# Three causal selects per head group, unscaled values and a newly searched instruction order in a gated attention and FFT kernel

## Chip, cores and metric

The kernel runs on one core of a Trainium2 chip. The metric is the device time of one execution, in microseconds (us), as the median of several runs. Three runs of the kernel before took 241.19, 241.27 and 241.69 us, a median of 241.27 us.

## The reference

The output is a mix of two branches over the same input rows (2048 tokens of 640 values). Branch A is attention in four segments of 512 tokens with 32 heads of 20 values; each segment attends causally to itself and reads a memory that the earlier segments have written. Branch B multiplies a two-dimensional FFT of the rows by weights. Cut to what matters:

```python
g = _sigmoid(beta).reshape(1, H, 1, 1)          # one gate per head
for s in range(N):                              # 4 segments of L = 512
    logits = einsum('bhqd,bhkd->bhqk', qs, ks) * Dh ** -0.5 + mask
    a_dot = einsum('bhqk,bhkd->bhqd', softmax(logits), vs)
    num = einsum('bhld,bhde->bhle', phi(qs), M)
    den = einsum('bhld,bhd->bhl', phi(qs), z)[..., None] + 1e-06
    o = g * (num / den) + (1.0 - g) * a_dot     # phi(t) = t + 1 if t > 0 else exp(t)
    M = M + einsum('bhld,bhle->bhde', phi(ks), vs)
    z = z + einsum('bhld->bhd', phi(ks))
a = concat(o) @ wo
b = irfft2(rfft2(x) * (w_r + 1j * w_i))
t = _sigmoid((x * gate_w).sum(-1))              # one gate per token
return t * a + (1 - t) * b
```

## The kernel before

**How the program is made.** `Kern.record()` writes down every operation with what it reads and writes; nothing is sent to an engine yet. `Sched.schedule` then goes through a long table of numbers, ORDER, which holds each engine's queue (so the order on TensorE, VectorE, ScalarE, GpSimd and SyncE is written by hand, or rather by a search), and gives the PSUM banks out while it walks along. Where an operation may run on two engines (`copy_alts`: ScalarE or VectorE, `either` and `small`: VectorE or GpSimd), the table also chooses the engine. A second table, ENDED, ranks the operations by the end that was once found for them; `emit` uses the rank when it writes the waits. `either` and `small` carry `lock`, by which the scheduler's model holds VectorE off while GpSimd works. The table decides the order alone; the times in the model appear nowhere in the machine's program.

**Names of the stages.** `project` makes q, k and v of a segment out of the transposed rows xT. q and k are copied out of PSUM (qu, q0), stored to qk_scr and loaded again as padded blocks (qkp); phi of both is made by an exp on ScalarE (et, L1201) and two VectorE operations (phq and phk, L1213 and L1214). v comes out of `vproj` and is written to va by VectorE, times 1 - g of its head (L1244, `ev_v`); odd tiles of 128 tokens are stored with their two halves of 64 partitions exchanged, which the vproj matmuls do by 64-column pieces. The same matmuls give the token gate's sum, which ScalarE turns to exp (L1242).

**Attention.** The heads go in eight groups of four. Of two groups, five QK units go to PSUM (`UNITS`: a and b of the first group, a of the second, one unit c for both, b of the second). Every unit fills all four banks 0 to 3, so the next unit's matmuls wait for the exp of this one (L1393, ScalarE), which writes ex, of which there are three copies (NEX). Masking is done on ex by GpSimd's affine select (L1414), seven times per group: four of 128x256, one of 128x512 and two of 64x512 elements, each issued when the exp of its unit is there. Then the PV matmuls follow (va by ex): for segments 0 to 2 transposed (`pv_flipped`), and the sums stand beside the outputs in PSUM; for segment 3 `pv_group`, where the division is made per tile (L1450, L1453, L1455).

**The denominators of segments 0 to 2.** The unnormalised outputs are copied out of PSUM (ub), stored to u_scr, and the row of sums is loaded back as a 128x128 block (dnc). VectorE takes the reciprocal (dnr, L1340), multiplies it by the token gate gcc (rc, L1342), rc is stored to r_scr and loaded, spread over the head columns, as r4. The outputs are loaded back from u_scr as oU in five pieces, multiplied by r4 (L1656), the memory's part mT is added (L1664), and oU is multiplied by wo, in the same PSUM bank as branch B's last stage. All transfers are issued by SyncE (L555, transposing ones L553) except a few on ScalarE. The last such chain, that of segment 2, stands beside segment 3's attention.

**Helpers of the trace.** All matmuls are recorded by two lines (L521; L519 for those that are split into 32-column pieces), all copies by two (L530 on ScalarE, L532 on VectorE). Stages of branch B appear as Ac, Bt, Pt, Yt, Cp and eo, G (L1615) being its last sum.

## Time and profile before

| what | number |
|---|---|
| median of three runs | 241.27 us |
| profiled execution, from first to last instruction | 247.9 us |
| its granted TensorE clock, mean | 0.972 |
| TensorE, ScalarE, VectorE, GpSimd busy | 93%, 81%, 79%, 67% |
| exps on ScalarE | 92, together 138.7 us |
| affine selects on GpSimd | 224, together 121.0 us |

The profile gives no other time for its execution than the span of 247.9 us; it is 6.6 us above the median of the timed runs, so one profiled microsecond stands for a little less than one of the metric. In the views, a row names line, engine and operation with output and inputs (numbers of buffers left out), how often it stands there, the busy time and the mean of one in ns; what stands behind the bar is the idle time of the engine just before and what ended it. In the chain of waits each row is a start, a length and the piece of work that the end was waiting for at that time. The execution is cut by eye into a start (until about 13.5 us, where the first exp begins), a long stretch of exps (until about 174.3 us, the 60th exp) and a tail.

### The profile page before, as it was taken

Reading aid. Unit: us, or ns where it says so; the run is one execution under the profiler, and the core shown is the slowest. Engines: PE = TensorE matmul, PEld = TensorE weight load, DVE = VectorE, ACT = ScalarE, POOL = GpSimd, SP = SyncE. Lnnn points to the kernel's source line nnn. Section 1 sums busy time; section 2 is a strip of 40 time slices with the busy share of each in tenths; the row PEclk is TensorE's granted clock in tenths of the full one; section 3 lists DMA queues with packets and bytes.
Section 4 is the critical chain, followed back from the end, with each engine's and each line's share of the span. In section 5 each row is a group of like instructions: output and inputs, shape, how many; then the busy total and the mean of one; then the engine's idle time right before and its main releaser. Section 6 shows DMA issues by size and latency. Waiting matters only on the chain.

```text
span 247.9 us, 9233 instructions
## 1 busy us (share of the span) xinstructions
PE 230.0 (93%) x3849; PEld 139.7 (56%) x3849; DVE 196.3 (79%) x481; ACT 199.7 (81%) x241; POOL 165.7 (67%) x297
## 2 busy tenths in 40 slices
PE   7899999999999999998899999999999975699994
PEld 2574667765465665545566554455444543366794
DVE  0489998799999987888998979979888831755653
ACT  2289688998999989999999899999999864278740
POOL 8532278367969658478939998949898660559640
PEclk9999999999999999999999999999999995599999
DMA  7999979937875864768697543447665977382123
GB/s 174 281 361 206 229 191 230 269 91 203 222 173 163 199 213 114 206 95 252 170 242 208 165 131 99 122 146 192 188 183 128 282 101 81 35 118 81 59 81 109
DMA packets 58924, 42.11 MB, mean 170 GB/s; under 512 B 30020, under 2 KB 55172, under 8 KB 58884
## 3 DMA queue, kind: packets, MB, share of 16 engines
q1 hardware_dynamic: 57844, 40.96, 66.4%
q8 instruction: 30, 0.49, 0.8%
q10 hardware_dynamic: 1040, 0.57, 0.8%
q14 instruction: 10, 0.08, 0.2%
HBM read 23.32 MB, written 12.30 MB: 144 GB/s over the span
## 4 chain that ended last, share of the span: by engine, by line
PE 59%; DVE 15%; DMA 12%; ACT 8%; SPq 3%; issue 2%; DVEq 0%
PE psum L521 52%; PE psum L519 6%; ACT ex L1393 5%; DMA r<-r_scr 3%; DMA r_scr<-rc 3%; DVE Pt L1569 3%; DMA Wt<-in_B_w_i_dram 2%; DMA wk<-in_A_wk_dram 2%; DMA qk_scr<-qu 2%; SPq L553 2%; DVE G L1615 1%; SPq L555 1%; DVE oU L1656 1%; DVE phk L1213 1%; DVE va L1244 1%
## 5 line engine op out<-in xcount | busy, mean ns | idle before, releaser
L1393 ACT ACTIVATE ex<-psum 128x2048 bf16<-128x2048 f32 (+4 forms) x92 | 138.7, 1507 | 13.2 <-PE psum L521 11.4
L1414 POOL TENSOR_SCALAR_AFFINE_SELECT ex<-ex 128x256 bf16<-128x256 bf16 (+2 forms) x224 | 121.0, 562 | 41.2 <-ACT ex L1393 38.3
L521 PE MATMUL psum<-qkp 20*64 20x64 bf16 (+5 forms) x1024 | 31.8, 268 | 4.0 <-ACT ex L1393 2.1
L521 PE MATMUL psum<-xT,wk 128*128 128x256 bf16 (+1 forms) x280 | 33.9, 273 | 0.6 <-DMA wk<-in_A_wk_dram 0.6
L521 PE MATMUL psum<-xT,wq 128*128 128x512 bf16 (+1 forms) x135 | 30.7, 381 | 0.5 <-DMA xT<-in_A_x_dram 0.5
L521 PE MATMUL psum<-wv,xT 128*64 128x320 bf16 (+3 forms) x240 | 30.1, 303 | 0.3 <-DVE va L1244 0.3
L1569 DVE TENSOR_TENSOR Pt<-psum,Wt 128x642 bf16<-128x642 f32 x32 | 25.5, 821 | 2.6 <-PE psum L521 1.5
L521 PEld LDWEIGHTS psum<-qkp 20*64 20x64 bf16 (+1 forms) x1024 | 12.2, 101 | 22.0 <-ACT ex L1393 14.8
L521 PEld LDWEIGHTS psum<-xT,wk 128*128 128x128 bf16 (+1 forms) x280 | 19.9, 97 | 7.1 <-DMA wk<-in_A_wk_dram 1.6
L519 PE MATMUL psum<-wo,oU 128*32 128x320 bf16 x480 | 23.5, 317 | 0.2 <-DVE oU L1664 0.2
L1035 POOL TENSOR_TENSOR xsb<-xf 128x320 bf16<-128x320 bf16 (+2 forms) x12 | 9.5, 788 | 16.2 <-DVE xsb L1035 12.2
L1244 DVE TENSOR_TENSOR va<-psum,ebx 128x320 bf16<-128x320 f32 x32 | 15.2, 483 | 5.0 <-ACT gate L1242 2.9
L521 PEld LDWEIGHTS psum<-wv,xT 128*64 128x64 bf16 (+1 forms) x240 | 14.9, 105 | 7.4 <-issue 2.9
L532 DVE CAST ot<-psum 128x320 bf16<-128x320 f32 x21 | 10.1, 491 | 11.2 <-PE psum L519 8.8
L521 PE MATMUL psum<-big,Cp 128*128 128x321 bf16 (+1 forms) x96 | 18.7, 310 | 0.2 <-DVE G L1615 0.2
L521 PE MATMUL psum<-big,Ac 128*128 128x160 bf16 (+2 forms) x96 | 18.1, 257 | 0.3 <-DVE Pt L1569 0.2
L521 PE MATMUL psum<-ex,va 128*32 128x512 bf16 (+4 forms) x480 | 17.3, 275 | 0.5 <-DVE mem L1289 0.2
L521 PE MATMUL psum<-tt,Yt 128*128 128x256 bf16 (+1 forms) x96 | 16.5, 276 | 1.1 <-DVE Pt L1569 0.4
L1615 DVE TENSOR_TENSOR G<-eo,psum 128x320 bf16<-128x320 f32 x32 | 14.7, 482 | 3.5 <-PE psum L521 2.5
L1201 ACT ACTIVATE et<-qu 128x512 bf16<-128x512 bf16 x25 | 15.6, 629 | 0.2
L519 PEld LDWEIGHTS psum<-wo,oU 128*32 128x32 bf16 x480 | 12.5, 100 | 5.7 <-issue 1.1
L521 PEld LDWEIGHTS psum<-ex,va 128*32 128x32 bf16 x480 | 10.1, 96 | 9.8 <-POOL ex L1414 1.7
(99 smaller groups left out, 393.7 us busy)
## 6 DMA issues: line engine op xcount, KB each, us to landing
qkp<-qk_scr SPq DMA_DIRECT2D x28, 160.0 KB
tt<-tab_tt SPq DMA_DIRECT2D x8, 512.0 KB, 3.8
qk_scr<-qu SPq DMA_DIRECT2D x12, 256.0 KB, 2.4
u_scr<-ub SPq DMA_DIRECT2D x12, 256.0 KB, 4.4
xsb<-in_A_x_dram SPq DMA_DIRECT2D x8, 320.0 KB, 5.9
oU<-u_scr SPq DMA_DIRECT2D x15, 128.0 KB, 4.0
out_dram<-ot SPq DMA_DIRECT2D x12, 160.0 KB
Wt<-in_B_w_r_dram SPq DMA_DIRECT2D x16, 80.2 KB, 3.3
```

Of the source, the lines that this page charges most:

```text
L519: h = e.matmul(dst, wt, r_, start=st, stop=sp_, **{**kw, "tile_position": (0, q), "skip_group_check": True})
L521: h = e.matmul(o_, l_, r_, start=st, stop=sp_, **kw)
L532: alts["dve"] = (lambda e: e.tensor_copy(dst(), src()), 67 + 1.04 * n, 68.0)
L553: return e.dma_start_transpose(d_, s_)
L555: return e.dma_start(d_, s_)
L1035: self.either(lambda e, dst=dst, src=src, d0=d0, n=n, op=op: e.tensor_tensor(xs.ap(o + dst, [D, 2], [1, n]), xf.ap(src + d0, [321, 2], [1, ...
L1201: self.one("act", lambda e: e.activation(et.ap(0, [1, L]), qsl(), ACT.Exp), L, [qb], [b("et", pi_)], late, name="phi_exp")
L1244: self.one("dve", lambda e: e.tensor_tensor(va.ap(i * H * VW + h0 * VW, [VW, nh], [1, DH]), self.ps(bank, 0, [DH, nh], [1, DH]), self.ebx. ...
L1393: self.one("act", lambda e, d=d, q=q: e.activation(self.ex.ap(*d), self.ps(bank, *q), ACT.Exp, scale=SC), n, [bank], [self.exb(s, 2 * pr + ...
L1414: self.one("pool", lambda e: e.affine_select(self.ex.ap(e0 + d0, [1280, 4], [1, n], np_=np_), self.ex.ap(e0 + s0, [1280, 4], [1, n], np_=np_),
L1569: self.one("dve", lambda e, ri=ri, Pt=Pt, Wt=Wt, wo_=wo_, bank=bank: e.tensor_tensor(Pt.ap(ri * 322, [644, 2], [1, KD]), self.ps(bank, 0, ...
L1615: self.one("dve", lambda e, q=q, n2=n2, bank=bank, eo=eo: e.tensor_tensor(self.G.ap(n2 * D + 639 * q, [1 - 2 * q, 320]), eo.ap(q, [1, 320] ...
```

## The change

Five things are changed.

- **Selects.** The layout of ex is changed so that the masked pieces lie at equal distances, and three selects take the place of seven: mask_first (128 x 512 elements), mask_odd (64 x 1024) and mask_even (128 x 1024). They are recorded once per group, behind the unit c or the last unit b. The sum of elements per partition is kept; the QK matmuls of kind b have 64 output rows instead of 128, so QK has 1536 instead of 1024 matmuls. In segment 3 exps are no longer split for the layout: 80 instead of 92.
- **Values.** v is copied to va without a factor, by ScalarE or VectorE (`copy_alts`): 21 copies go to ScalarE and 27 to VectorE, where 32 multiplications on VectorE stood. The exchange of halves in odd tiles is made by two 64-partition copies each; the vproj matmuls are 160 full ones in place of 240, and the token gate's exps 16 in place of 24.
- **The factor 1 - g** goes elsewhere: into rc for segments 0 to 2 (omp, one column of 1/(1 + exp(beta)) per partition, by a scalar_tensor_tensor), into a table g3 for segment 3, and ebg is built from 1 + exp(beta) accordingly.
- **Rank.** ENDED is gone; the rank of an operation is its end in the scheduler's own walk.
- **ORDER** is another table throughout. It also chooses engines anew: of the q and k copies qu VectorE has 19 instead of 13 and ScalarE 11 instead of 17, and eight of the sums xsb of branch B's input that stood on GpSimd go to VectorE.

```diff
-    def schedule(self, pools, order, ended, nsem=56):
+    def schedule(self, pools, order, nsem=56):
-        for i, v in enumerate(ended):
-            ops[v].rank = i
...
+        for i, o in enumerate(sorted(ops, key=lambda o: o.t1)):
+            o.rank = i
...
-    PIECES = (((0, 0, 0, 0, 0, 512), (1, 64, 64, 128, 0, 64), (0, 64, 64, 64, 64, 448)),
-              ((1, 0, 0, 192, 0, 320), (2, 0, 0, 320, 320, 192)),
-              ((2, 0, 0, 256, 0, 64), (3, 64, 64, 384, 0, 128), (3, 0, 0, 448, 64, 64)))
+    PIECES = (((0, 0, 0, 0, 0, 512), (1, 64, 64, 128, 0, 64), (0, 64, 64, 64, 64, 448)),
+              ((2, 0, 0, 256, 0, 256), (3, 64, 64, 384, 0, 64), (2, 64, 64, 320, 64, 192), (1, 0, 0, 256, 256, 256), (1, 64, 64, 256, 256, 256)),
+              ((1, 0, 0, 192, 0, 64), (1, 64, 64, 192, 0, 64), (3, 0, 0, 448, 256, 64), (3, 64, 64, 448, 256, 64)))
...
-        46, 0, 90, 26, 74, 23, 2, 4, 36, 24, 6, 8, 28, 10, 12, 72, 14, 16, 30, 18, 20, 178, 64, 34, 202, 66, 68, 44, 42, 70, 93, 214, 52, 190, 48, 94,
+        23, 0, 80, 26, 2, 4, 24, 6, 8, 28, 10, 12, 98, 84, 14, 112, 82, 16, 30, 18, 20, 34, 222, 198, 46, 186, 210, 48, 40, 188, 224, 212, 200, 190,
...
+        self.one("act", lambda e: e.activation(self.omp.ap(0, [1, 1]), self.betp.ap(0, [1, 1]), ACT.Exp), 1, [b("betp")], [b("omp")], 1.0)
+        self.one("dve", lambda e: e.tensor_scalar(self.omp.ap(1, [1, 1]), self.omp.ap(0, [1, 1]), 1.0, None, ALU.add), 1, [], [b("omp")], 1.0)
+        self.one("dve", lambda e: e.reciprocal(self.omp.ap(2, [1, 1]), self.omp.ap(1, [1, 1])), 1, [], [b("omp")], 1.0)
...
-        self.one("dve", lambda e: e.tensor_tensor(
-            va.ap(i * H * VW + h0 * VW, [VW, nh], [1, DH]), self.ps(bank, 0, [DH, nh], [1, DH]),
-            self.ebx.ap(H + h0, [1, nh], [0, DH]), ALU.mult), nh * DH, [bank, b("omgh")], [vb], prio, name="ev_v")
+        for p0, p1, n in ((0, 64, 64), (64, 0, 64)) if i % 2 else ((0, 0, P),):
+            self.Sc.op(self.copy_alts(lambda p0=p0, n=n: va.ap(i * H * VW + h0 * VW, [VW, nh], [1, DH], p0=p0, np_=n),
+                                      lambda p1=p1, n=n: self.ps(bank, 0, [DH, nh], [1, DH], p0=p1, np_=n), nh * DH),
+                       r=[bank], w=[vb], prio=prio, name="ev_v")
...
-        self.one("dve", lambda e: e.tensor_tensor(self.rc.ap(0, [1, P]), self.dnr.ap(0, [1, P]), self.gcc.ap(0, [1, P]), ALU.mult), P,
-                 [b("dnr"), b("gcc")], [b("rc")], prio, name="den_gate")
+        self.one("dve", lambda e: e.scalar_tensor_tensor(self.rc.ap(0, [1, P]), self.dnr.ap(0, [1, P]), self.omp.ap(2, [1, 1]), self.gcc.ap(0, [1, P]),
+                                                              ALU.mult, ALU.mult), P,
+                 [b("dnr"), b("gcc"), b("omp")], [b("rc")], prio, name="den_gate")
...
-            if ks == "a":
-                self.mask(s, g, P, 512, 0, 64, ("a0",), ("m1",), prio, 64)
-                self.mask(s, g, P, 0, 0, P, (), ("a0",), prio, 0)
-            elif ks == "b":
...
+        if u == 3:
+            self.mask(s, 2 * pr, prio)
+        elif u == 4:
+            self.mask(s, 2 * pr + 1, prio)
...
+        x = [self.exb(s, g, k) for k in ("a0", "b0", "c0", "m0")]
+        self.one("pool", sel(512, 0, 64, 64, P), 512, x[:2], x[3:], prio, per=0.793, fix=218, name="mask_first")
+        self.one("pool", sel(512, 512, P, -64, 64), 1024, [], x[2:], prio, per=0.793, fix=218, name="mask_odd")
+        self.one("pool", sel(0, 0, P, 0, P), 1024, [], x[:2], prio, per=0.793, fix=218, name="mask_even")
```

Three places of the new order follow. The first is SyncE's queue around the last denominator chain: dnc is the row of sums that is loaded back, r_scr the store of rc, r42 the load of it that the normalisation waits for. Before:

```order
L555 DMA dnc_122<-u_scr 128x1x128
L553 DMA_TRANSPOSE mT2_81<-o_scr 128x5x128
L555 DMA oU1_112<-u_scr 128x1x512
L555 DMA wo2_85<-in_A_wo_dram 128x5x640
L555 DMA g_scr<-gT_135 4x16x8
L555 DMA qkp1_104<-qk_scr 20x8x512
L553 DMA_TRANSPOSE mT1_80<-o_scr 128x5x128
L555 DMA oU2_113<-u_scr 128x1x512 x5
L555 DMA r_scr<-rc_123 128x128
L555 DMA out_0_dram<-ot0_74 4x32x640
L555 DMA qkp1_104<-qk_scr 20x8x512
```

The same stretch after (the diff shifts the lines, so L553 is the issuing line now):

```order
L553 DMA u_scr<-ub1_121 128x2x512
L553 DMA oU2_113<-u_scr 128x1x512 x2
L553 DMA dnc_122<-u_scr 128x1x128
L553 DMA qkp1_104<-qk_scr 20x8x512 x2
L553 DMA gbc_70<-g_scr 128x512
L551 DMA_TRANSPOSE mT2_81<-o_scr 128x5x128
L553 DMA r_scr<-rc_123 128x128
L553 DMA qkp1_104<-qk_scr 20x8x512
L553 DMA out_0_dram<-ot0_74 4x32x640
L553 DMA oU2_113<-u_scr 128x1x512
L553 DMA r42_93<-r_scr 128x1x512
L553 DMA oU2_113<-u_scr 128x1x512 x2
```

Between dnc and the store of rc there stood eleven transfers, among them the 800 KB of wo2 and all five pieces of oU2; after the change four stand there, two pieces of oU2 are ahead of dnc, one follows the store and two follow the load of r42. The second place is TensorE where segment 2's outputs oU2 are first multiplied, ahead of the QK unit c of the last two groups but one. Before:

```order
L521 MATMUL psum_52<-G_56,fbg2_73 32x320 x4
L519 MATMUL psum_52<-wo2_109,oU1_112 32x320 x4
L519 MATMUL psum_52<-wo0_107,oU2_113 32x320 x4
L519 MATMUL psum_52<-wo3_110,oU1_112 32x320 x4
L519 MATMUL psum_52<-wo4_111,oU1_112 32x320 x4
L519 MATMUL psum_52<-wo1_108,oU2_113 32x320 x4
L521 MATMUL psum_52<-qkp1_104 64x64 x4
```

And after:

```order
L519 MATMUL psum_52<-G_56,fbg2_73 32x320 x4
L517 MATMUL psum_52<-wo0_107,oU2_113 32x320 x4
L517 MATMUL psum_52<-wo1_108,oU2_113 32x320 x4
L517 MATMUL psum_52<-wo2_109,oU2_113 32x320 x4
L519 MATMUL psum_52<-qkp1_104 64x64 x32
L517 MATMUL psum_52<-wo3_110,oU2_113 32x320 x4
```

The first oU2 matmuls keep their place relative to that QK unit (which has 32 matmuls of 64x64 now, where 24 stood). The third place is the start of ScalarE's queue, where the table exp of beta (ebx) stood. Before:

```order
L1007 ACTIVATE ebx_131<-beta_130 128x32
L530 ACTIVATE qkp0_103<-psum_52 128x512 x3
L1393 ACTIVATE ex_114<-psum_52 128x4x512
L530 ACTIVATE q0_69<-psum_52 128x512 x3
L1201 ACTIVATE et0_97<-q0_69 128x512
```

And after:

```order
L528 ACTIVATE qkp0_103<-psum_52 128x512 x2
L1260 ACTIVATE ex_114<-psum_52 128x4x512
L1082 ACTIVATE et1_98<-q0_69 128x512
L528 ACTIVATE q0_69<-psum_52 128x512
L1260 ACTIVATE ex_114<-psum_52 128x4x512
L1082 ACTIVATE et0_97<-q0_69 128x512
L528 ACTIVATE va0_105<-psum_52 128x16x20
L528 ACTIVATE va0_105<-psum_52 64x16x20
```

The exp of beta is not among the first operations any more, and the copies of v stand between the first exps. On SyncE the load of wk has moved up accordingly: it is second, behind one transposed load of xT, where a load of xsb, the same load of xT and that of beta stood ahead of it.

110 lines of the change are left out of this document (43 added, 67 removed), and 305 rows, old and new, of tables (ENDED, ORDER).

## The prediction

> **What bounds the kernel now.** I read the page's table of engines first, then its chain of waits by engine:
>
> ```profile
> PE 230.0 (93%) x3849; PEld 139.7 (56%) x3849; DVE 196.3 (79%) x481; ACT 199.7 (81%) x241; POOL 165.7 (67%) x297
> PE 59%; DVE 15%; DMA 12%; ACT 8%; SPq 3%; issue 2%; DVEq 0%
> ```
>
> TensorE is busy for 93% of the span and GpSimd, from which the change takes most, isn't in the chain at all. Averages over stages hide where the time is, so the second view is busy time by stretch (columns: stretch, length, then busy us and count of PE, PEld, DVE, ACT, POOL, the granted clock, the DMA share, GB/s):
>
> ```profile
> 0.00:13.50 13.50, 11.05 (x154) 5.57 (x155) 4.42 (x9) 3.13 (x6) 8.81 (x13) 1.00 0.91 240
> 13.50:174.30 160.80, 156.08 (x2201) 93.49 (x2199) 146.30 (x359) 148.77 (x179) 112.87 (x208) 1.00 0.72 186
> 200.50:213.40 12.90, 6.36 (x138) 3.78 (x126) 4.83 (x14) 4.95 (x6) 3.77 (x6) 0.63 0.48 64
> 213.40:247.90 34.50, 31.26 (x868) 22.86 (x868) 18.72 (x45) 19.01 (x24) 17.76 (x31) 0.94 0.42 87
> ```
>
> In the long stretch three engines are nearly full: of 160.8 us VectorE has 14.5 free and ScalarE 12.0. GpSimd has 47.9. The hole is the third row here: in 12.9 us TensorE works 6.4, at a clock of 0.63. The third view, the chain of waits in order of time, names its cause:
>
> ```profile
> 195.92 6.75 DMA r_scr<-rc
> 202.69 7.07 DMA r<-r_scr
> 209.78 1.77 DVE oU L1656 x5
> 212.45 0.94 DVE oU L1664
> 213.43 1.26 PE psum L519 x16
> ```
>
> The last denominator chain: the store of rc takes 6.75 us, its load back 7.07, then five normalisations, then the addition, and at 213.43 TensorE gets its oU2. Its beginning stands in the timelines of SyncE and VectorE:
>
> ```profile
> 182.29 0.56 SPq L555 DMA_DIRECT2D u_scr<-ub  x1
> 187.12 0.51 SPq L555 DMA_DIRECT2D dnc<-u_scr  x1
> 189.64 0.60 SPq L555 DMA_DIRECT2D wo<-in_A_wo_dram  x1
> 192.69 3.18 SPq L555 DMA_DIRECT2D oU<-u_scr  x5
> 195.92 0.60 SPq L555 DMA_DIRECT2D r_scr<-rc  x1
> 189.45 0.94 DVE L1340 RECIPROCAL dnr<-dnc 128x128 f32<-128x128 bf16 x1
> 192.65 0.47 DVE L1342 TENSOR_TENSOR rc<-dnr,gcc 128x128 bf16<-128x128 f32 x1
> ```
>
> From the issue of u_scr (182.29) to TensorE (213.43) it is 31.1 us. rc is ready at 193.12, but SyncE is busy with five loads of oU2 until 195.87, and the 800 KB of wo were put into the rings 6 us earlier.
>
> **Term 1, the last chain.** Counted from the issue of u_scr. dnc waits for its landing, 4.83 us as before; two oU2 loads now stand ahead of it, at 3.18 / 5 = 0.64 each: issue at 6.1. Landing up to dnr took 2.33 (187.12 to 189.45): 8.4; the reciprocal 0.94: 9.4. Ahead of rc then stand one G, one eo and a small rs; their rows are
>
> ```profile
> L1615 DVE TENSOR_TENSOR G<-eo,psum 128x320 bf16<-128x320 f32 x32 | 14.7, 482 | 3.5 <-PE psum L521 2.5 <-ACT eo L530 0.8
> L532 DVE COPY eo<-psum 128x321 f32<-128x321 f32 x6 | 2.9, 479 | 0.0
> L1450 DVE TENSOR_TENSOR rs<-psum,gate 128x16 f32<-128x16 f32 x8 | 1.4, 169 | 1.9 <-PE psum L521 1.9
> ```
>
> 1.1 together, and rc 0.47: 11.0, where r_scr is issued without the five loads ahead of it, and without wo's 800 KB. Its landing has no row free of these; the nearest are the landings of the loads of r and of oU:
>
> ```profile
> DMA to landing us min/median/max: 2.5/4.8/7.1
> DMA to landing us min/median/max: 2.5/4.0/4.7
> ```
>
> (the first of r, three loads; the second of oU, fifteen). The store lies between 2.5 and the 6.75 that it took; I take oU's median 4.0, since three transfers to two still stand close ahead: 15.0. The load of r lies between 2.5 and 7.1; I take its median 4.8: 19.8. From there it was 3.65 to TensorE; three normalisations do for the first matmuls, and two of 1.77 / 5 go: 2.9. The sum is 22.7 instead of 31.1: **-8.4**. With the landings of before it is 28.5 (-2.6). With 2.5 for both it would be 18.9, but there TensorE's own work decides: of that third row's stretch it is idle 12.9 - 6.4 = 6.5 us, and some 4.3 of the rest run at half clock, so that without any pause it would be there 6.5 + 2.2 = 8.7 sooner, at 22.4. The forecast therefore has the chain and TensorE arrive together. Another 1.7 us would come from the half clock behind 213.4 (some 3.4 us of work). Range of the term: -10.4 to -2.6.
>
> **Term 2, ScalarE.** What it gains and loses:
>
> ```profile
> L530 ACT ACTIVATE ot<-psum 128x320 bf16<-128x320 f32 x11 | 4.7, 436 | 10.7 <-PE psum L519 8.1 <-PE psum L521 1.7 <-DMA out_dram<-ot 0.8
> L530 ACT ACTIVATE qu<-psum 128x512 bf16<-128x512 f32 x17 | 10.1, 596 | 2.7 <-PE psum L521 2.0 <-DMA qk_scr<-qu 0.5
> L1242 ACT ACTIVATE gate<-psum 64x1 f32<-64x1 f32 x16 | 2.6, 165 | 0.6 <-PE psum L521 0.2
> ```
>
> A copy of v is of ot's shape: 21 x 0.436 = +9.2. Six copies qu leave, -3.6; two q of like size, -1.2; one Ac and one Bt, -1.1; eight small gate exps, -1.3. With one ub more (+0.6) and a little less for exps the stretch gets 2.5 longer, if none of it falls into ScalarE's 12 idle us: **+2.5**, between 0 and 2.5.
>
> **Term 3, VectorE.** It loses 32 multiplications and gets 27 copies of the same width (the half ones cost as much, since elements per partition count), five ot go:
>
> ```profile
> L1244 DVE TENSOR_TENSOR va<-psum,ebx 128x320 bf16<-128x320 f32 x32 | 15.2, 483 | 5.0 <-ACT gate L1242 2.9 <-PE psum L521 1.8
> L532 DVE CAST qu<-psum 128x512 bf16<-128x512 f32 x13 | 8.9, 683 | 0.7 <-PE psum L521 0.5
> L1035 DVE TENSOR_TENSOR xsb<-xf x20: 310/324/844, 9.0 to 34.9; 128x320 bf16<-128x320 bf16 x8, 128x318 bf16<-128x318 bf16 x6, 128x322 bf16<-128x322 bf16 x6
> ```
>
> Five va and four ot less, -4.4; six qu +4.1, two q +1.4, eight xsb from GpSimd +2.6, four eo +1.9; the smaller groups (oTl, Bt, Ac, additions to on, one ub less) about +2.6. That is +8.2 against 14.5 us of free time. I take a quarter, **+2.0**, since waits fill up with work before it reaches the path; between 0 and 8.2.
>
> **Term 4, the selects.** The waits by line and their durations:
>
> ```profile
> POOL ex L1414 <- ACT ex L1393: 38.3, 31, 3.7
> PEld psum L521 <- POOL ex L1414: 1.7, 6, 0.4
> L1414 POOL TENSOR_SCALAR_AFFINE_SELECT ex<-ex 128x256 bf16<-128x256 bf16 x128 | 59.5, 476 | 38.7 <-ACT ex L1393 37.4
> L1414 POOL TENSOR_SCALAR_AFFINE_SELECT ex<-ex 64x512 bf16<-64x512 bf16 x64 | 42.6, 670 | 1.8 <-ACT ex L1393 0.9
> L1414 POOL TENSOR_SCALAR_AFFINE_SELECT ex<-ex 128x512 bf16<-128x512 bf16 x32 | 22.0, 690 | 0.6
> ```
>
> GpSimd waits for exps; TensorE waits for selects 1.7 us in all. The slope is (690 - 476) / 256 = 0.84 ns per element, so one of 1024 takes about 1.12 us, and a group 0.69 + 2 x 1.11 = 2.9 us instead of 3.9. None of the 33 us that GpSimd saves over 32 groups comes to the end, as the chain has none of it. But all three now start after the group's last exp, 2.9 us up to PV instead of one 0.67-us select; PV has three ex buffers of slack: **+0.8**, between 0 and the 2.2 of one such delay at the end.
>
> **Term 5, the start.** The first matmuls wait for wk (chain of waits):
>
> ```profile
> 6.33 5.36 DMA wk<-in_A_wk_dram
> ```
>
> The order issues wk behind one load instead of three; two issues of half a us are saved: **-1.0**, between 0 and -1.8. **Term 6, QK**: 512 matmuls more of the same column time,
>
> ```profile
> L521 PE MATMUL psum<-qkp 20*64 20x64 bf16 (+5 forms) x1024 | 31.8, 268 | 4.0 <-ACT ex L1393 2.1
> ```
>
> 31 ns of TensorE's time each now. Their columns stay, so at most some tenth of that, 3 ns, is new per matmul by my choice: **+0.3**, between 0 and 512 x 3 ns = 1.6. The 80 vproj matmuls that go were half ones: nothing. The two new columns omp are made once, outside every path: nothing. rc as scalar_tensor_tensor has no row; I take rc's 0.47, and twice that would be 0.5 more.
>
> Sum: -8.4 + 2.5 + 2.0 + 0.8 - 1.0 + 0.3 = **-3.8** against the profiled 247.9. That span lies 6.6 above the median; taken off the median, 241.27 - 3.8 = **237.5 us**.
>
> [...] The granted clock, by stretches of a us:
>
> ```profile
> 201.00:202.00 1.00, 0.00 (x0) 0.00 (x0) 0.82 (x2) 0.44 (x1) 1.00 (x3) 1.00 0.28 87
> 204.00:205.00 1.00, 1.00 (x20) 0.68 (x17) 0.00 (x0) 1.00 (x1) 0.00 (x0) 0.50 0.52 156
> ```
>
> TensorE stood still from about 200.6 to 202.6, for a load of qkp, and from 203.4 it had half its clock, which lasted beyond 213.4. A pause of 2 us was enough, and one of that kind may well stay; so the sum takes no gain from the 1.7 us behind 213.4. [...]
>
> [...]
>
> ```profile
> L1213 DVE TENSOR_SCALAR phq<-qu x15: 273/283/712, 34.7 to 157.4; 128x512 bf16<-128x512 bf16 x15
> L1213 DVE TENSOR_SCALAR phq<-qu 128x512 bf16<-128x512 bf16 x15 | 5.3, 363 | 0.0
> ```
>
> These operations on SBUF take up to 0.43 us longer than their median of 283 ns, about the length of one short select, and 0.08 us longer in the mean. [...]
>
> **Rivals.**
> A, the chain goes as forecast and the long stretch isn't longer (terms 2 and 3 fall into idle time): -8.4 + 0.8 - 1.0 + 0.3 gives 233.0. For it: 12.0 and 14.5 idle us. Against: TensorE, ScalarE and VectorE wait for each other in turn.
> B, slower: VectorE becomes the bound of the long stretch. All 8.2 us of term 3 count instead of 2.0: -8.4 + 2.5 + 8.2 + 0.8 - 1.0 + 0.3 = +2.4, 243.7. It turns slower as soon as more than 5.8 of the 8.2 are on the path. (If the landings stay as slow as before as well, 5.8 more, 249.5.) For it: VectorE at 146.3 of 160.8. Against: its waits.
> [...]
> D, the change's order brings r no sooner (its transfers queue elsewhere): +4.6, 245.9. Against: the five loads and wo are out of the way in the order.
>
> **How the numbers follow.** Forecast (235 to 239.5) 0.50; A 0.17; B 0.20; C 0.08; D 0.05. A measurement here can tell about 0.2%. Faster holds the forecast, A and a little of C: 0.68; same 0.06; slower B, D and the rest of C: 0.26. The range leaves out the far end of A and B: 231 to 245.5.
>
> **What would show it.** u_scr to the first oU2 matmul at about 23 us, r landing with TensorE idle for under 2 us ahead of them; the long stretch 3 to 5 us longer, with ScalarE and VectorE over 93% busy; selects three per group at 0.69 and 1.1 us; the first exp about 1 us sooner. Wrong if the hole before the first oU2 matmul is there again at full length, or if the stretch from the first to the 60th exp isn't longer, or is longer by over 6 us.

## The result and the profile after

The changed kernel takes **249.16 us** (median of four runs, 246.75 to 252.29), the kernel before beside it 241.23 us. The ratio is 1.028, with a 95% interval of 1.022 to 1.033: the change makes the kernel slower by 2.8%. (Ratios, here and below, are taken from the fast runs alone, those not more than 1.5% above the kernel's fastest, so they aren't the quotients of the medians beside them.) The forecast was 237.5 us and faster.

A single later run of a kernel says little here (the kernel before gave 240.9 to 249.3 us in 22 runs on one chip), so both kernels were run and profiled once more, unchanged:

| | before, first profile | before, again | after | after, again |
|---|---|---|---|---|
| runs, median (us) | 241.27 | 242.16 (10 runs) | 249.16 (4) | 249.13 (4) |
| ratio to before | | 1.000 (0.996 to 1.004) | 1.028 (1.022 to 1.033) | 1.025 (1.013 to 1.037) |
| span of the profiled execution | 247.9 | 241.3 | 244.8 | 247.1 |
| time of that same execution | not shown | 243.28 | 246.75 | 248.99 |

The last two rows bring a correction of what is said on the profile of before: a span lies 1.9 to 2.0 us **below** the time of its execution (1.7 to 2.9 in all 399 executions of the runs below that have both). The first profile's 247.9 us therefore belong to an execution of about 249.8 us (an estimate), some 8.6 us above the median. (That a profiled microsecond stands for a little less than one of the metric is wrong, then.) It was an unusual execution, and no ruler for a typical one. "Before" below is the second profile.

The page's engines, of the kernel after:

```profile
PE 227.7 (93%) x4281; PEld 142.3 (58%) x4281; DVE 200.3 (82%) x496; ACT 198.3 (81%) x231; POOL 132.3 (54%) x164
PE 63%; ACT 13%; DVE 12%; DMA 4%; SPq 3%; issue 2%; POOL 2%; DVEq 0%; ACTq 0%
```

GpSimd does 33 us less, as forecast, and is 2% of the chain of waits. Where the time went is read from busy time by stretch. The cuts are at the same work in both kernels: the first exp, the end of the 60th exp of before (the 59th after the change, since one split exp is whole there), and the start of the exp of the QK unit that is the 70th of 80. Columns: stretch, length, busy us of PE, PEld, DVE, ACT, POOL, clock, DMA share, GB/s. Before:

```profile
0.00:13.73 13.73, 11.29 (x154) 5.49 (x155) 4.27 (x9) 3.09 (x5) 8.81 (x13) 1.00 0.92 241
13.73:174.12 160.39, 154.72 (x2189) 94.04 (x2199) 146.34 (x359) 148.46 (x179) 112.46 (x208) 1.00 0.78 187
174.12:198.38 24.26, 23.33 (x445) 12.36 (x445) 21.09 (x55) 21.96 (x29) 20.61 (x37) 1.00 0.78 198
198.38:241.30 42.92, 36.59 (x1057) 27.14 (x1055) 24.12 (x60) 25.67 (x31) 23.48 (x40) 1.00 0.51 93
```

After, first profile:

```profile
0.00:11.17 11.17, 9.23 (x145) 4.75 (x146) 1.71 (x3) 2.38 (x4) 5.14 (x9) 1.00 0.84 209
11.17:172.40 161.23, 154.97 (x2518) 96.42 (x2515) 150.71 (x379) 150.59 (x185) 91.69 (x119) 1.00 0.77 191
172.40:198.09 25.69, 23.09 (x484) 12.57 (x484) 22.80 (x54) 20.75 (x22) 18.82 (x20) 1.00 0.78 191
198.09:244.80 46.71, 40.46 (x1143) 28.54 (x1141) 25.07 (x62) 24.57 (x25) 16.66 (x17) 0.91 0.50 87
```

After, again:

```profile
0.00:11.31 11.31, 9.30 (x142) 4.54 (x142) 1.71 (x3) 2.37 (x3) 5.14 (x9) 1.00 0.83 203
11.31:173.44 162.13, 154.08 (x2505) 96.59 (x2518) 150.70 (x379) 150.68 (x185) 91.72 (x119) 1.00 0.78 190
173.44:199.69 26.25, 23.10 (x484) 12.57 (x484) 23.28 (x54) 20.83 (x21) 18.91 (x20) 1.00 0.74 189
199.69:247.10 47.41, 39.07 (x1143) 28.25 (x1140) 24.76 (x62) 24.38 (x25) 16.54 (x17) 0.96 0.50 86
```

Length after minus before, row by row: -2.6 (-2.4 in the second profile), +0.8 (+1.7), +1.4 (+2.0), +3.8 (+4.5). The sums are +3.5 and +5.8, the differences of the spans. TensorE's busy time in the two middle rows is the same within 0.7 us; what grew there is idle time. In the last row the two profiles differ in kind. In the first, TensorE is idle as long as before (46.71 - 40.46 = 6.25 us against 6.33), but its clock is 0.91, and the work takes 3.9 us longer. In the second it is idle 2.0 us longer (8.34) and at a clock of 0.96. So nearly all of the loss lies behind the long stretch, and part of it is clock.

The last denominator chain, on which the forecast's large term rested, in the chain of waits of before:

```profile
194.98 3.54 DMA r_scr<-rc
198.53 4.11 DMA r<-r_scr
202.67 1.77 DVE oU L1656 x5
205.38 1.10 DVE oU L1664
```

There is no hole: the landings take 3.54 and 4.11 us, where the unusual execution had 6.75 and 7.07. The DMA packets of that execution say what its hole was: 14 packets of 256 bytes hung at the same time for 2.7 to 3.2 us each, all from 206.6 to 209.7, and r landed at their end; r_scr landed just behind a shorter group of the kind (16 packets, up to 2.6 us, until 202.45). The same will be met again in the tail after the change. SyncE issued u_scr at 182.11, and TensorE's timeline has its first oU2 matmuls at 206.13, so the chain takes 24.0 us and not 31.1:

```profile
206.13 1.12 PE L519 MATMUL psum<-wo,oU 128*32 128x320 bf16 x20
```

After, SyncE's timeline and TensorE's (what stands in brackets is the idle time before):

```profile
183.22 0.37 SPq L553 DMA_DIRECT2D u_scr<-ub  x1
194.52 0.36 SPq L553 DMA_DIRECT2D r_scr<-rc  x1
196.62 0.60 SPq L553 DMA_DIRECT2D r<-r_scr  x1
```

```profile
206.69 0.99 PE L517 MATMUL psum<-wo,oU 128*32 128x320 bf16 x12 [1.01 <-DVE oU L1522]
```

That is 23.5 us: 11.3 up to r_scr, 13.4 up to the load of r. The gain is 0.5 us. But the transfers no longer set the end of this chain. r lands 2.9 us after its issue, at 16.3, and VectorE starts the five normalisations only at 19.2: in its queue two copies ot stand ahead of them, which wait for TensorE. Then all five normalisations and the addition of mT come first (tile view of r, VectorE's timeline):

```profile
DMA to landing us min/median/max: 2.9/2.9/2.9
201.56 0.89 DVE L530 CAST ot<-psum 128x320 bf16<-128x320 f32 x2 [1.86 <-PE psum L517]
202.37 2.14 DVE L1514 TENSOR_TENSOR oU<-oU,r 128x512 bf16<-128x512 bf16 x5
204.54 2.09 DVE L1522 TENSOR_TENSOR oU<-oU,mT 128x640 bf16<-128x640 bf16 x2
```

TensorE itself waits for the chain for 1.0 us and would have been there at 22.5, so against the 24.0 of before there was at most 1.5 us to gain.

### The profile page after: what moved, and what is told of

It reads as the page before. It is cut to its first block, busy times and chain, and to the rows that moved or that the text cites. A ratio compares the mean times of both kernels' runs of the same rounds, so it can differ in the third digit from the quotient of the medians.

```text
span 244.8 us, 9960 instructions
## 1 busy us (share of the span) xinstructions
PE 227.7 (93%) x4281; PEld 142.3 (58%) x4281; DVE 200.3 (82%) x496; ACT 198.3 (81%) x231; POOL 132.3 (54%) x164
## 4 chain that ended last, share of the span: by engine, by line
PE 63%; ACT 13%; DVE 12%; DMA 4%; SPq 3%; issue 2%; POOL 2%; DVEq 0%; ACTq 0%
PE psum L519 56%; ACT ex L1260 10%; PE psum L517 7%; SPq L553 2%; DMA wk<-in_A_wk_dram 2%; DMA qk_scr<-qu 1%; DVE va L530 1%; DMA wo<-in_A_wo_dram 1%; ACT va L528 1%; POOL ex L1272 1%; DVE Pt L1427 1%; SPq L551 1%; DVE xf L907 1%; DVE oU L1514 1%; DVE oU L1522 1%
## 5 line engine op out<-in xcount | busy, mean ns | idle before, releaser
L1260 ACT ACTIVATE ex<-psum 128x2048 bf16<-128x2048 f32 (+1 forms) x80 | 136.5, 1707 | 18.4 <-PE psum L519 15.9
L1272 POOL TENSOR_SCALAR_AFFINE_SELECT ex<-ex 128x1024 bf16<-128x1024 bf16 (+2 forms) x96 | 90.5, 956 | 55.9 <-ACT ex L1260 54.7
L519 PE MATMUL psum<-qkp 20*64 20x64 bf16 (+4 forms) x1536 | 33.1, 255 | 5.1 <-ACT ex L1260 4.2
L519 PEld LDWEIGHTS psum<-qkp 20*64 20x64 bf16 x1536 | 14.8, 104 | 25.1 <-ACT ex L1260 20.1
L519 PE MATMUL psum<-wv,xT 128*128 128x320 bf16 (+1 forms) x160 | 29.1, 300 | 0.1
L519 PEld LDWEIGHTS psum<-wv,xT 128*128 128x128 bf16 x160 | 14.5, 97 | 6.6 <-ACT va L528 0.7
L519 PE MATMUL psum<-ex,va 128*32 128x256 bf16 (+2 forms) x480 | 17.2, 274 | 0.2 <-POOL ex L1272 0.2
L517 PEld LDWEIGHTS psum<-wo,oU 128*32 128x32 bf16 x480 | 12.9, 102 | 7.5 <-issue 1.7
L519 PE MATMUL psum<-big,Ac 128*128 128x161 bf16 (+2 forms) x96 | 16.7, 257 | 0.5 <-DVE Ac L530 0.2
L1432 POOL TENSOR_TENSOR Yt<-Pt 128x321 bf16<-128x321 bf16 x17 | 12.7, 758 | 7.4 <-PE psum L519 4.9
L519 PE MATMUL psum<-tt,Yt 128*128 128x256 bf16 (+1 forms) x96 | 15.7, 275 | 0.3 <-DVE qu L530 0.2
L530 DVE CAST va<-psum 64x320 bf16<-64x320 f32 (+1 forms) x27 | 13.2, 488 | 2.1 <-ACT va L528 0.7
```

The source lines that it names most:

```text
L517: h = e.matmul(dst, wt, r_, start=st, stop=sp_, **{**kw, "tile_position": (0, q), "skip_group_check": True})
L519: h = e.matmul(o_, l_, r_, start=st, stop=sp_, **kw)
L530: alts["dve"] = (lambda e: e.tensor_copy(dst(), src()), 67 + 1.04 * n, 68.0)
L1260: self.one("act", lambda e: e.activation(self.ex.ap(*d), self.ps(bank, *q), ACT.Exp, scale=SC), n, [bank], [self.exb(s, 2 * pr + gp, ks) f ...
L1272: return lambda e: e.affine_select(self.ex.ap(e0 + d0, [640, 8], [1, n], np_=np_), self.ex.ap(e0 + s0, [640, 8], [1, n], np_=np_), [[0, 8] ...
L1432: fn = lambda e, r=r, a0=a0, a1=a1, op=op, Pt=Pt, Yt=Yt: e.tensor_tensor(Yt.ap(r * 322, [1, KD]), Pt.ap(a0 * 322, [1, KD]), Pt.ap(a1 * 322 ...
```

## Experiments

**The kernels as they are.** These are the first two of the columns above.

> The kernel before, unchanged. Theory 1 (the hole belonged to the one profiled execution, not to the kernel): the three spans are about 239 us, 8 to 9 us below the 247.9 of the first profile, and the long pause of TensorE ahead of the first oU2 matmul (4.8 us, with half clock behind it) is missing or under 2 us. Theory 2 (the hole is the kernel's, and a profiled execution is just longer): the spans are near 247 us, with r_scr and r landing 6 to 7 us after their issue.

> The changed kernel, unchanged. Theory 1: spans 245 to 250 us as in the first four runs, so 6 to 9 us above the kernel before in the same runs, and the stretches up to the 61st exp and behind it tell where they differ. Theory 2: the same spans as the kernel before within 3 us.

What they gave stands above. The runs that follow are called e1 to e16, in the order in which they were made. They took the large term out of the sum: the span of before was 241.3 us where theory 1 had named 239, and its pause ahead of the first oU2 matmul is gone.

**Order and code apart.** Three kernels join parts of the two. The tables were carried over entry by entry, since the operations' numbers differ. First, all of the change in before's order:

```diff
-        23, 0, 80, 26, 2, 4, 24, 6, 8, 28, 10, 12, 98, 84, 14, 112, 82, 16, 30, 18, 20, 34, 222, 198, 46, 186, 210, 48, 40, 188, 224, 212,
+        48, 0, 98, 26, 82, 23, 2, 4, 36, 38, 24, 6, 8, 28, 10, 12, 80, 14, 16, 30, 18, 20, 186, 66, 34, 210, 68, 70, 46, 44, 72, 74, 76, 78,
```

> All of the change except the order table: three selects, unscaled v on the engines that the change chose for it, 1536 QK matmuls, the factor in rc; every engine's queue is that of the kernel before, with the selects of a group where its last old select stood and a copy of v where its multiplication stood. If the new order costs the time: about as fast as the kernel before, 240 to 243 us. If the pieces cost it (longer selects that hold VectorE, 21 more copies on ScalarE, more QK matmuls): 246 us or more, like the changed kernel.

**e1**: 278.76 us, ratio 1.136 (1.121 to 1.150). Second, before's code in the change's order:

```diff
-        46, 0, 90, 26, 74, 23, 2, 4, 36, 24, 6, 8, 28, 10, 12, 72, 14, 16, 30, 18, 20, 178, 64, 34, 202, 66, 68, 44, 42, 70, 93, 214, 52,
+        23, 0, 72, 26, 2, 4, 24, 6, 8, 28, 10, 12, 90, 76, 14, 104, 74, 16, 30, 18, 20, 34, 36, 214, 190, 44, 178, 202, 46, 38, 180, 216,
```

> The opposite: the code of the kernel before (seven selects, v scaled by VectorE, 1024 QK matmuls), in the order of the change, the seven selects where the three stand. If the new order costs the time: 246 to 252 us, with the loss behind the 51st exp as in the changed kernel. If the pieces cost it: 239 to 243 us.

**e2**: 261.32 us, ratio 1.072 (1.062 to 1.083). Both lie far above what either theory had named. Third, before with the selects, their layout and the QK pieces alone, in before's order:

```diff
-        return [self.exb(s, g, k) for k in ("a0", "b0", "b1", "c0", "m1", "m3")]
+        return [self.exb(s, g, k) for k in ("a0", "b0", "c0", "m0")]
...
+        self.one("pool", sel(512, 0, 64, 64, P), 512, x[:2], x[3:], prio, per=0.793, fix=218, name="mask_first")
+        self.one("pool", sel(512, 512, P, -64, 64), 1024, [], x[2:], prio, per=0.793, fix=218, name="mask_odd")
+        self.one("pool", sel(0, 0, P, 0, P), 1024, [], x[:2], prio, per=0.793, fix=218, name="mask_even")
```

> The kernel before with the three selects, the new layout of ex, unsplit exps and 1536 QK matmuls alone; v, its factor and the old order stay. If selects or QK cost the time (lock, PE instructions): 245 us or more, and e1 the same. If not: within 1.5 us of the kernel before, faster if anything since segment 3 has 12 exps less.

**e3**: 265.52 us, ratio 1.082 (1.069 to 1.096). Its engines, its waits and its phq operations:

```profile
PE 234.6 (88%) x4347; PEld 143.9 (54%) x4361; DVE 205.2 (77%) x481; ACT 199.1 (75%) x229; POOL 139.6 (53%) x169
```

```profile
PEld psum L519 <- POOL ex L1265: 19.2, 16, 2.0
PE psum L519 <- POOL ex L1265: 14.3, 14, 1.7
```

```profile
L1084 DVE TENSOR_SCALAR phq<-qu x15: 271/285/1174, 35.8 to 168.9; 128x512 bf16<-128x512 bf16 x15
```

Before has the same 481 VectorE operations, whose busy time is shorter, and the longest phq is shorter too (page and tile view of before):

```profile
PE 225.9 (94%) x3837; PEld 139.0 (58%) x3849; DVE 195.8 (81%) x481; ACT 199.2 (83%) x241; POOL 165.4 (69%) x297
```

```profile
L1213 DVE TENSOR_SCALAR phq<-qu x15: 271/283/714, 35.0 to 157.2; 128x512 bf16<-128x512 bf16 x15
```

Two things are to be seen. PV now waits for the selects, which start after the group's last exp (14.3 us for matmuls; before, the weight loads' 1.7 us were the longest such entry). And VectorE's same operations take 9.4 us longer, single ones up to 0.46 us more than the longest of before. Summed one by one, those that touch SBUF alone take 8.4 us longer and those that read PSUM 0.4. This lengthening of VectorE's operations on SBUF beside GpSimd's selects is what the expectations call the lock, and what C stands for in the forecast's chances. With their layout and the QK pieces, three selects cost some 20 us in before's order (by the ratio); in the order made for them the waits are gone (below). So neither half of the change is good without the other, and the old order is no neutral place to test a piece of it.

The rank by itself:

```diff
-        for i, v in enumerate(ended):
-            ops[v].rank = i
...
+        for i, o in enumerate(sorted(ops, key=lambda o: o.t1)):
+            o.rank = i
```

> The kernel before with the rank of the operations by their end in the scheduler's own walk, the ENDED table left out, nothing else. All theories expect no difference: within 0.5% of the kernel before, since the rank decides only in which order an instruction's waits are written.

**e4**: 242.76 us, ratio 0.999 (0.995 to 1.004): it does nothing that can be measured.

**The change's pieces, in the change's order.** The two-by-64 QK pieces were joined where they are one block of 128 keys, 1152 matmuls instead of 1536:

```diff
-              (..., (1, 0, 0, 256, 256, 256), (1, 64, 64, 256, 256, 256)),
-              ((1, 0, 0, 192, 0, 64), (1, 64, 64, 192, 0, 64), (3, 0, 0, 448, 256, 64), (3, 64, 64, 448, 256, 64)))
+              (..., (1, 0, 0, 256, 256, 256, P)),
+              ((1, 0, 0, 192, 0, 64, P), (3, 0, 0, 448, 256, 64, P)))
```

> The changed kernel with neighbouring QK matmuls of 64 keys joined to one of 128 where they write the same columns: 1152 in place of 1536, so 768 instructions less for TensorE (matmuls and weight loads) and three 16-KB instruction loads less. If TensorE's instructions (or the loads of them) are what is late: 2 to 4 us less than the changed kernel, 243 to 246. If not: the same within 1 us.

**e5**: 246.53 us, ratio 1.015 (1.009 to 1.020). That is 1.1 to 1.3% below the change's own two ratios; the interval lies clear of the first of these and not of the second. So 384 small matmuls are worth up to some 3 us, where term 6 had priced 512 of them at 0.3 to 1.6. Then each select of 1024 elements was issued as two of 512:

```diff
-            return lambda e: e.affine_select(self.ex.ap(e0 + d0, [640, 8], [1, n], np_=np_), ...
+            for h in range(0, n, 64):
+                r = e.affine_select(self.ex.ap(e0 + d0 + h, [640, 8], [1, 64], np_=np_), ...
```

> The changed kernel with each select of 1024 elements written as two of 512, in the same place: one lasts 0.69 instead of 1.1 us, so VectorE is held shorter at a time, while GpSimd works 0.5 us more per group. If the length of the lock costs the time: 1 to 4 us less than the changed kernel. If PV waits for the last select: up to 3 us more. If neither: the same within 1 us.

**e6**: 247.92 us, ratio 1.024 (1.018 to 1.030), the same as the change: in its own order the length of the selects costs nothing that shows.

All 48 copies of v on VectorE (21 numbers of the table are changed to the other engine):

```diff
-        114, 420, 482, 506, 108, 508, 484, 422, 315, 424, 510, 426,
+        114, 420, 482, 506, 108, 508, 485, 422, 315, 424, 511, 426,
```

> The changed kernel with all 48 copies of v on VectorE, in the places where they stand: ScalarE has 9.2 us less, VectorE 10.2 us more. If ScalarE bounds the long stretch (term 2 of the prediction): 1 to 2.5 us less than the changed kernel. If VectorE does (rival B): 3 to 10 us more.

**e14**: 256.45 us, ratio 1.058 (1.053 to 1.064). The stretch from the first exp to the 70th unit, of this kernel, and in the change's second profile:

```profile
11.36:209.41 198.05, 179.99 (x2988) 109.51 (x3002) 184.76 (x453) 164.18 (x183) 109.37 (x138) 0.99 0.73 180
```

```profile
11.31:199.69 188.38, 177.19 (x2988) 109.16 (x3002) 173.98 (x432) 171.51 (x205) 110.63 (x138) 1.00 0.78 190
```

VectorE has 10.8 us more to do there, ScalarE 7.3 less, and the stretch is 9.7 longer. In this order VectorE's room is used up: more work on it goes to the end almost whole. Whether an order searched for 48 copies on VectorE would do better was not tried.

**The tail.** The two rows behind the long stretch hold three events. Each was taken away, shortened or filled with other work.

*The wait for wo.* In the second profile TensorE waits 1.5 us for 160 KB of wo (the wait by line; 0.4 us in the first profile, 1.8 and 1.9 in e5 and e6), and the chain passes through that load:

```profile
PE psum L517 <- DMA wo<-in_A_wo_dram: 1.5, 1, 1.5
```

```profile
182.89 3.17 DMA wo<-in_A_wo_dram
```

Its issue was moved ahead of three transfers, as SyncE's queue shows:

```diff
 L553 DMA oU_112<-u_scr 128x1x512 x2
+L553 DMA wo_110<-in_A_wo_dram 128x1x640
 L553 DMA gbc<-g_scr 128x512
 L551 DMA_TRANSPOSE mT_81<-o_scr 128x5x128
 L553 DMA u_scr<-ub_120 128x2x512
-L553 DMA wo_110<-in_A_wo_dram 128x1x640
```

> The changed kernel with one entry of SyncE's queue moved: the load of the fourth piece of wo (128 rows of 640) stands three transfers earlier, ahead of the store of ub that waits for its copy. If TensorE's wait for it (0.4 and 1.5 us in the two profiles, at 184 us) is on the path: that much less, 0.5 to 1.5 us. If it only moves the wait elsewhere: the same.

**e8**: 246.07 us, ratio 1.011 (1.005 to 1.017). The wait is gone; between 181 and 188 us TensorE works 6.01 us where the change's second profile has 5.23. The ratio is 1.4 to 1.7% below the change's own two, some 3.4 to 4.1 us, clear of the first one's interval and not of the second's. That is more than the 0.5 to 1.5 us expected and more than the wait itself; where the rest comes from isn't shown. Together with the joined QK pieces:

> The changed kernel with both edits that gained: the load of wo's fourth piece earlier (e8) and the joined QK matmuls (e5). If they take away different losses (a wait for a transfer, and TensorE's instructions): the gains add, 2.5 to 5 us less than the changed kernel, 243 to 245 us, within 1% of the kernel before. If both only take away the same pause: no less than e8, 246 us.

**e9**: 245.29 us, ratio 1.013 (1.008 to 1.019): no better than the move alone, so the gains don't simply add.

*The pause and the clock.* Ahead of the first oU2 matmuls TensorE waits 1.0 us for the addition of mT (the bracket in the row at 206.69 above). That addition took 1683 ns beside one of 1693 ns on GpSimd, against 492 in the median (tile view, second profile after); whether it would take the pause away to put GpSimd's one on VectorE was not tried:

```profile
L1522 DVE TENSOR_TENSOR oU<-oU,mT x7: 479/492/1683, 189.3 to 231.5; 128x640 bf16<-128x640 bf16 x7
L1522 POOL TENSOR_TENSOR oU<-oU,mT x1: 1693/1693/1693, 206.2 to 206.2; 128x640 bf16<-128x640 bf16 x1
```

During it, at 206.1, the clock falls in the first profile after (the second has the same pause of 1.0 us and no fall at it):

```profile
204.00:208.00 4.00, 2.99 (x96) 1.90 (x93) 3.99 (x12) 1.88 (x1) 1.69 (x1) 0.76 1.41 86
208.00:212.00 4.00, 4.00 (x74) 2.04 (x68) 1.34 (x4) 2.46 (x3) 0.79 (x1) 0.50 0.40 82
```

To keep the array busy there, one group of four matmuls was issued eight times over (the repeats write the same values to the same bank):

```diff
+            if (s, a, hf) == (2, 0, 0):
+                items = items * 8
```

> The changed kernel with the four matmuls of branch B's last stage ahead of segment 2's first oU2 matmuls issued eight times over (same values, start flag set): about 1 us of dense TensorE work in the place where it pauses for 1.0 us. If the lost clock behind that pause is the loss: granted clock 0.99 or more in most runs and 2 to 3 us less than the changed kernel. If it isn't: the same or up to 1 us more, clock as before (0.98 to 0.99).

**e7**: 249.04 us, ratio 1.022 (1.014 to 1.030). A miss: the group chosen ran at 211.21 us, behind the pause, and the clock fell at 207.3 as before. With the right group, and wo moved:

```diff
+            if len(self.Sc.ops) == 2052:
+                items = items * 8
```

> e8 with the four matmuls of branch B's last stage issued eight times at the pause itself, ahead of the first oU2 matmuls (e7 repeated another group of the same four, that ran at 211 us, behind the pause). TensorE's array gets 0.9 us of full work in the window of 3.41 us that lies ahead of the fall at 206 us, raising its use from 0.34 to about 0.6. If the clock falls behind a window of little use: no fall at 206 us in the profile and a clock that isn't below e8's, 1 to 3 us less than e8. If it falls behind any pause: as in e8 or 1 us more.

**e10**: 245.37 us, ratio 1.008 (1.004 to 1.012), no clear gain on e8's 1.011. The fall at 206 is gone from its profile (of an execution of 247.54 us). Another pause follows, in its chain of waits, and the clock falls behind that one, at 213.2:

```profile
209.06 3.95 issue
```

*The standstill.* That pause has no releaser ("issue": the engine waits for nothing that the profile shows). The second profile after has the like, in its waits of the stretch 200 to 216 us:

```profile
DVE oU L1522 <- DMA mT<-o_scr: 4.6, 1, 4.6
PE psum L519 <- issue: 2.4, 1, 2.4
```

There, 17 packets of 256 bytes begin between 208.5 and 209.0 and take 4.1 to 4.6 us each, until 213.1. (The expectation of e11, below, speaks of all 16 DMA rings. That is too much: the records name no ring, and 264 other packets, of 4 to 1280 bytes, begin and land between 209 and 213.) The transposing load mT lands at 215.5. The next load of instructions, by their number TensorE's own (the trace has 34 of 16 KB for 8562 matmuls and weight loads, that of before 30 for 7686; here they come every 3.5 to 5.5 us), starts at 213.16, 9.1 us after the one before, and TensorE stops from 213.25 to 215.65 in the middle of a QK unit. That the late load causes the stop is a guess from the times: in e5 and e9, with joined QK pieces, such a stop of 0.9 and 0.4 us ends ahead of the next load, and the two profiles with the clock down by then, the change's first and e8, have none. SyncE's timeline of the same execution shows what was issued ahead of it:

```profile
204.71 0.52 SPq L553 DMA_DIRECT2D g_scr<-gT  x1
206.66 2.57 SPq L551 DMA_TRANSPOSE mT<-o_scr  x1
```

g_scr is a store in pieces of 4 bytes. It was moved behind the transposing load:

```diff
-L553 DMA g_scr<-gT 4x16x8
 L553 DMA out_dram<-ot_75 4x32x640
 L551 DMA_TRANSPOSE mT_80<-o_scr 128x5x128
+L553 DMA g_scr<-gT 4x16x8
```

> The changed kernel with one entry of SyncE's queue moved: the last store of the token gate (g_scr, 2 KB in 4-byte pieces) stands behind the transposing load of mT instead of two places ahead of it. In all profiles of the change all 16 DMA rings stand still for 3 to 4.7 us at about 207 to 213 us, beginning 3.8 us after that store and about 2 us after that load; mT and TensorE's next 16 KB of instructions land only behind it. If the store ahead of the transposing load causes the standstill: it is gone from the profile, and the median is 1.5 to 4 us below the changed kernel's, 245 to 247 us. If the transposing load causes it alone: the standstill is there as before and the time the same within 1 us.

**e11**: 245.83 us, ratio 1.017 (1.012 to 1.022), 0.8 to 1.1% below the change's own two; the interval just touches the first one's and lies within the second's. SyncE's timeline there:

```profile
206.95 1.21 SPq L551 DMA_TRANSPOSE mT<-o_scr  x1
208.20 0.47 SPq L553 DMA_DIRECT2D g_scr<-gT  x1
```

The longest packet there takes 1.7 us instead of 4.6, the transposing load's issue 1.21 us instead of 2.57, and TensorE works through the window from 211 to 215 us, of this kernel and then of the change:

```profile
211.00:215.00 4.00, 4.00 (x114) 2.74 (x110) 0.99 (x3) 3.42 (x3) 1.96 (x3) 1.00 0.23 73
```

```profile
211.00:215.00 4.00, 2.25 (x54) 1.29 (x44) 0.00 (x0) 2.12 (x2) 1.75 (x2) 1.00 0.47 99
```

The other way round, in before the store was moved behind that of r_scr, so that it stands close ahead of the transposing load:

```diff
-DMA g_scr<-gT 4x16x8
 DMA qkp_104<-qk_scr 20x8x512
 DMA_TRANSPOSE mT_80<-o_scr 128x5x128
 DMA oU_113<-u_scr 128x1x512 x5
 DMA r_scr<-rc 128x128
+DMA g_scr<-gT 4x16x8
```

> The kernel before (as in e4) with the last store of the token gate moved behind the store of rc, so that a store of ot, a load of qkp and a transposing load of mT follow it, the last about 2 us behind it, as in the change. If a 4-byte store some 2 us ahead of a transposing load makes the rings stand still: a standstill of over 3 us from about 199 us in the profile, a late load of r, and 1 to 5 us more than the kernel before. If the standstill belongs to something else in the change: as e4, 242 to 243 us.

**e13**: 243.91 us, ratio 1.007 (1.003 to 1.010), a little slower, but no standstill: the longest packets took 2.67 us, as in before (2.70). So the pair of store and transposing load doesn't make it by itself. It is a matter of degree: at this place the longest packet takes 3.1 to 4.8 us in the nine profiles of the change's own order with the store in its place, and 1.7 to 2.5 in the four with it moved, the kernel above and three more below. That moving the store shortens it is shown; what brings it about stays open.

*All together.* The joined QK pieces, wo and g_scr in one kernel; the same with the filling of the pause; and the two moves without the joined pieces:

> e9 (wo earlier, joined QK matmuls) with the same move of the gate's store. If the standstill is a loss of its own: 2 to 3 us below e9, 242 to 243 us, level with the kernel before. If e9 has already taken away what hangs on it: as e9, 245 us.

> e12 with the filling of e10 at the pause of 0.9 us ahead of the first oU2 matmuls. If lost clock is what is left between e12 and the kernel before: 1 to 2 us less than e12, 242 to 243 us, with a clock of 0.997 or more as in the kernel before. If not: the same or 1 us more, since the filling is work.

> The changed kernel with the two moves in SyncE's queue alone (wo's fourth piece earlier as in e8, the gate's store later as in e11), QK matmuls as in the change. If these two transfers hold all of the loss: as e12, 243 to 245 us. If the 768 additional TensorE instructions cost something of their own: 1 to 2 us above e12, 245 to 246 us.

**e12**: 244.13 us, ratio 1.004 (1.000 to 1.008). **e15**: 243.99 us, 1.005 (1.001 to 1.009). **e16**: 244.99 us, 1.013 (1.008 to 1.017). Three small edits take back some 2.1 to 2.4 of the 2.5 to 2.8%. The two moves without joined pieces gain no more than wo alone, so the 384 matmuls that the change could do without cost some 0.8% here; and the filling adds nothing where the standstill is short. No kernel here beat the one before.

How much of it is clock can be estimated from the runs behind the ratios: span x (1 - granted clock), in the mean, is 3.6 us in the change's first runs and 2.0 in its later ones (three each), 0.5 for before beside the latter (ten runs); 2.1 with wo moved, 2.2 with g_scr moved, 1.1 with all three, 0.2 with the filling as well. (It counts half clock behind the last matmul too, about 1 us in e12's profile, which costs nothing.) So the clock is some 1.5 to 3 us of a loss of 6 to 7, idle time and matmuls the rest.

## Why the prediction was wrong

**The step that failed is the ruler of term 1**, and behind it the last line of the sum, "That span lies 6.6 above the median; taken off the median". The 31.1 us from u_scr to TensorE were those of one execution that was itself 8.6 us slower than the median; I subtracted a gain measured in it from a median that never had the loss. In a typical execution of before the chain takes 24.0 us. So there was little to gain: **-0.5 instead of -8.4**. That the chain after the change came out near the forecast (22.7, measured 23.5) is in part luck. Its first half was right: r_scr issued at 11.0 (measured 11.3). Then r was there at 16.3 and not at 19.8, as the two landings took at most 2.1 and 2.9 us for the 4.0 and 4.8 taken; and the last part took 7.2 us for 2.9, since r waits in VectorE's queue, five normalisations come first and not three, and the addition is slowed by 1.2 us beside GpSimd. The mechanism acted, r came sooner, but the order of VectorE's queue took it back. rc took 1.23 us, with 0.47 taken and 0.5 more allowed for; its other two instances take 0.33, and selects of about 1.1 us stand beside it on GpSimd. A slip in the range: with the landings of before the chain is 11.0 + 6.75 + 7.07 + 2.9 = 27.7 and not 28.5, which has 3.65 at its end. The profile had given a warning that the forecast didn't use: 12.9 us with TensorE half idle and a clock of 0.63, in an execution that lay above all the timed ones.

**Terms 2 and 3, ScalarE and VectorE.** The work of ScalarE in the long stretch grew by 2.1 us (forecast 2.5), that of VectorE by 4.4 (forecast 8.2). The counted groups came out nearly as forecast (qu +3.9 for 4.1, va -2.0 for -2.4; a half copy of v costs as much as a whole one, 488 and 487 ns on VectorE, 430 and 435 on ScalarE); what the sum lacked is that phk and phq became 3.2 us shorter, presumably since GpSimd is busy for less time beside them (91.7 us in that stretch, where before has 112.5). The groups of after have phq at 305 ns in the mean, where 363 stood:

```profile
L1094 DVE TENSOR_SCALAR phq<-qu 128x512 bf16<-128x512 bf16 x15 | 4.5, 305 | 0.0
```

Both engines are about 93% busy there, as forecast. The stretch up to the 60th exp became 0.8 and 1.7 us longer, where terms 2, 3, 4 and 6 asked for 5.6: most of the work fell into idle time. Term 6 was too small: 384 matmuls fewer gain 2 us (e12 beside e16) to 3 us (e5).

**Term 4, selects.** Durations as forecast: three per group, 2.87 us, and TensorE hardly waits for them (page and waits of after):

```profile
L1272 POOL TENSOR_SCALAR_AFFINE_SELECT ex<-ex 128x1024 bf16<-128x1024 bf16 (+2 forms) x96 | 90.5, 956 | 55.9 <-ACT ex L1260 54.7
```

```profile
PEld psum L519 <- POOL ex L1272: 1.4, 5, 0.5
```

But the reason given, three ex buffers of slack, holds only in this order: in before's order the same selects cost some 20 us. **Term 5, the start**: -2.6 and -2.4 instead of -1.0, below the lower bound of -1.8.

**What was missing from the sum** is the rest of the tail: +1.4 and +2.0 us from the 60th exp to the 70th unit, +3.8 and +4.5 behind it, made of the wait for wo, the pause with its fall of the clock, and the standstill. None of them was an operation of the change; they came with its order. The sum put them at nothing. Without term 1 it would have been +4.6, or 245.9 us, and that is no better: of these +4.6 the start and the long stretch showed -1.8 and -0.7, and the tail +5.2 and +6.5.

**The rivals.** A is out. B's mechanism exists (v on VectorE: 10.8 us of work lengthened the stretch by 9.7), but the change stops short of its point. C stands for the time that VectorE's operations on SBUF lose beside GpSimd's selects, and that loss is measured: with the longer selects in before's order (e3) they make 8.4 of the 9.4 us that VectorE works longer. How it grows with the length of a select no run shows by itself; with the selects cut in two (e6, 1.024) the time was that of the change (1.028 and 1.025). The change's order keeps the loss small in sum: VectorE's operations on SBUF alone lie 6.1 to 6.6 us above their groups' medians, 8.5 to 9.2 before and 15.7 in e3; but the last chain meets it twice, in rc and in the addition of mT, about 2.1 us together. In number D (245.9) and above all the remark under B (249.5, slow landings as well) came near, and not by their reasons: r came sooner than forecast, and the long stretch grew by 0.8 to 1.7 us.

**The clock.** The forecast read the rows rightly: a pause of 2 us was enough (TensorE stood still from about 200.6 to 202.6, and in that profile the clock fell to half at 203.7, for 13.65 us). After the change 1.0 us was enough in four of the seven profiles with such a pause ahead of the first oU2 matmuls, and the other three kept their clock; so keeping the chain in step with TensorE does not by itself keep the clock.

## What to carry to other kernels

Before a hole in a profile is counted as a gain, compare the time of that execution with the timed runs: if it lies above all of them, the hole may not be in the median, and a second profile costs less than a wrong sum. Where an order is searched for the pieces that it holds, a piece tested in the other order tells of the mismatch and not of the piece; edit one thing inside the new order instead. In a tail with thin matmuls look for what the new queue order puts close together: short pauses, an operation that waits in a queue behind one that waits for another engine, and loads that now come just too late.
